# First batch of a fused attention and feed-forward kernel: k as fp32 over two hardware queues with casts on chip, first q in token quarters, v in three pieces

## The chip, the cores and the metric

One core of one Trainium2 chip. The metric is the device time of one execution in microseconds (us). Each kernel was run several times beside the kernel before on the same chip. The program runs on one core. A profiled span is about 1.8 us shorter than the device time of the same run.

## The reference, cut to what matters

```python
k_proj = np.einsum('ks,bhsd->bhkd', E, k)            # 64 projected rows per head
v_proj = np.einsum('ks,bhsd->bhkd', F, v)
scores = scale * np.matmul(q, k_proj.transpose(0, 1, 3, 2))
attn   = softmax(scores)
x      = np.matmul(attn, v_proj)                     # then heads side by side: (8192, 512)
g      = x @ w_gate                                  # 512 x 1536
out    = (g * sigmoid(g) * (x @ w_val)) @ w_out
```

There are 8 batches of 8 heads, 1024 tokens and head size 64, all fp32. The attention of a batch is small; the feed-forward matmuls make up 87% of the chain that ended last in the kernel before. It can't begin before the first batch has gone through projection, scores, softmax and the product with v.

## The kernel before

The kernel works in bf16. From the second batch on, attention is laid in between the feed-forward matmuls. The first batch has no such cover: k, q and v are loaded and cast by the Pool queue's transfers, and dummy matmuls on zeros (`warm`) keep the tensor engine running while they land.

```python
load_k(0, 0, 4)                      # Pool queue: fp32 in memory, bf16 in the tile
... E and F on the sync queue ...
load_k(0, 4, 8)
load_q(0, 0, 2)                      # heads 0-3, heads 4-7
load_v(0, (0, 4, 8))                 # two halves
load_w_gv(0, 1); load_w_gv(1, 2); load_w_gv(2, 4)
warm(8); turn(0); turn(1)            # turn: transpose E, then F, on the tensor engine
warm(7)
u_KV(0, "k", (0, 4), at="y")         # project k, heads 0-3
... u_KT: transpose it into the block-diagonal BD ...
u_KV(0, "k", (4, 8), at="y")
u_KT(0, at="v", prs=(2, 4))
u_T(0, 0, ...); u_T(0, 1, ...); u_T(0, 2, ...)     # transpose q
u_S(0, 0, "g"); ... u_S(0, 3, "a")   # scores and exp (exp on ACT)
u_R(0, 0); u_N(0, 0); ...            # row sums (DVE), products (Pool, two on DVE)
u_KV(0, "v", (0, 4), at="y")         # project v; BDV casts on ACT
u_A(0, 0, nc.scalar)                 # transpose the attention rows
...
u_KV(0, "v", (4, 8), at="y")
u_PV2(0, 0, 0, 0, nc.scalar); u_PV2(0, 0, 1, 0, nc.vector)   # product with v, xT copies
u_A(0, 1, nc.scalar); u_A(0, 3, nc.vector)
f_mm(0, 0, 0, 0)                     # first feed-forward matmuls, half width
```

The softmax here doesn't subtract the row's maximum and nothing guards it: scores larger than these inputs give would overflow.

## Time and profile before

| | kernel before |
|---|---|
| device time | 573.26 us (572.66 to 573.53, 4 runs) |
| tensor engine busy | 98% of a span of 572.4 us |
| second set of scores starts | 16.05 us |
| last piece of v lands | 20.0 us |
| first feed-forward matmul | 22.57 us |
| first gate matmul of full width ("the front") | 26.88 us |

The prediction below shows the lines. Two positions in the trace serve as rulers. The second score set (the first two sets together need all of k, and the attention transposes need both) says how the score chain does. The front, the first gate matmul with 512 columns, is where the tensor engine goes over to unbroken work; the rest of the span after it was 545.5 us here. The profiled run of the kernel before was one of its slower ones (574.16 us), 0.9 us above its median; if that lies ahead of the front, its front is late by as much.

### The profile page before, as it was taken

The page shows a single profiled execution, that of the slowest core. Times are in us where ns is not written, and L with a number is a line of the kernel's source. Part 1 is how long each engine was busy: PE and PEld are TensorE (multiplying, and loading weights), DVE is VectorE, ACT ScalarE, POOL GpSimd, SP SyncE. Part 2 cuts the span into 40 slices and gives each one's busy share as a digit, 9 for nine tenths or more (in the row PEclk, how much of TensorE's full clock was granted, in tenths as well). Part 3 has the DMA queues.
Part 4 walks back from the last instruction along what each step waited for, and adds up shares of the span by engine and source line. Part 5 has one row for each costly group of instructions (what it writes and reads, how often), then busy time and mean ns, then how long its engine had stood idle before and what let it go on. Part 6 is the DMA issues. An engine that isn't in the chain of part 4 may idle for free.

```text
span 572.4 us, 7867 instructions
## 1 busy us (share of the span) xinstructions
PE 561.2 (98%) x2910; PEld 268.6 (47%) x2967; DVE 336.8 (59%) x580; ACT 237.0 (41%) x416; POOL 107.9 (19%) x121
## 2 busy tenths in 40 slices
PE   8899999999999999999999999999999999999997
PEld 4654544444444444444444444444444444444444
DVE  2787566666466744766556665567546674554550
ACT  1655444353425434444335434354342543443232
POOL 6734131234002400124001330023200220000000
PEclk9999999999999999999999999999999999999999
DMA  9999993539901698037951399204990124100012
GB/s 160 196 200 206 201 161 74 93 64 196 201 37 41 110 190 157 18 75 129 187 108 38 59 179 195 63 22 88 197 176 37 42 52 74 38 37 25 31 39 92
DMA packets 105927, 61.34 MB, mean 107 GB/s; under 512 B 58016, under 2 KB 97696, under 8 KB 105888
## 3 DMA queue, kind: packets, MB, share of 16 engines
q0 software_dynamic: 42288, 29.89, 36.1%
q1 hardware_dynamic: 63312, 30.68, 25.1%
q8 instruction: 23, 0.38, 0.3%
q10 hardware_dynamic: 288, 0.26, 0.1%
q14 instruction: 16, 0.13, 0.1%
HBM read 60.29 MB, written 16.78 MB: 135 GB/s over the span
## 4 chain that ended last, share of the span: by engine, by line
PE 94%; DMA 2%; POOL 1%; ACT 1%; issue 1%; DVE 0%; POOLq 0%
PE yps L360 29%; PE vps L322 29%; PE gps L322 29%; PE kvp L147 3%; PE sc L227 2%; DMA vb<-in_v_dram 2%; PE pv L285 2%; PE aTp L274 0%; ACT xT L135 0%; PE qTp L193 0%; POOL kb L88 0%; PE kTp L172 0%; POOL qb L107 0%; ACT th L334 0%; PE pv L300 0%
## 5 line engine op out<-in xcount | busy, mean ns | idle before, releaser
L341 DVE SCALAR_TENSOR_TENSOR s<-th,gps 128x512 f32<-128x512 f32 x192 | 130.5, 680 | 138.0 <-ACT th L334 137.8
L322 PE MATMUL gps<-xT,wg 128*128 128x512 bf16 (+1 forms) x755 | 195.7, 377 | 1.2
L322 PE MATMUL vps<-xT,wv 128*128 128x512 bf16 (+1 forms) x761 | 195.9, 377 | 0.8
L360 PE MATMUL yps<-wo,hT 128*128 128x512 bf16 (+2 forms) x761 | 191.5, 376 | 0.8
L334 ACT ACTIVATE th<-gps 128x512 f32<-128x512 f32 x192 | 114.6, 597 | 162.6 <-PE gps L322 155.1
L346 DVE TENSOR_TENSOR hT<-s,vps 128x512 bf16<-128x512 f32 x192 | 132.0, 688 | 22.1 <-PE vps L322 1.5
L360 PEld LDWEIGHTS <-hT 128*128 128x128 bf16 x780 | 76.2, 98 | 89.9
L258 POOL TENSOR_TENSOR AAd<-ee,rr 128x512 bf16<-128x512 f32 x52 | 54.1, 1040 | 319.5 <-issue 168.4
L322 PEld LDWEIGHTS <-wv 128*128 128x128 bf16 x776 | 73.9, 98 | 82.9 <-issue 3.3
L322 PEld LDWEIGHTS <-wg 128*128 128x128 bf16 x776 | 74.0, 98 | 81.3 <-issue 0.6
L370 ACT ACTIVATE ysb<-yps 128x512 f32<-128x512 f32 (+1 forms) x65 | 38.4, 590 | 78.1 <-PE yps L360 74.4
L135 ACT CAST xT<-pv 128x512 bf16<-128x512 f32 x62 | 36.1, 585 | 51.3 <-PE pv L285 50.3
L242 DVE TENSOR_REDUCE zz<-ee 128x8 f32<-128x512 f32 x64 | 43.5, 679 | 17.9 <-ACT ee L231 17.9
L231 ACT ACTIVATE ee<-sc 128x512 f32<-128x512 f32 x64 | 37.9, 595 | 17.4 <-PE sc L227 17.4
L285 PE MATMUL pv<-AT,BDV 128*128 128x512 bf16 x60 | 22.6, 379 | 0.1
L227 PEld LDWEIGHTS <-qTd 128*128 128x128 bf16 x208 | 16.0, 98 | 12.3
L227 PE MATMUL sc<-BD,qTd 128*128 128x128 bf16 x208 | 20.1, 219 | 0.1
L135 DVE CAST BDV<-kvp 64x256 bf16<-64x256 f32 x14 | 6.0, 426 | 22.1 <-ACT ks L157 19.1
L258 POOL TENSOR_TENSOR AA<-ee,rr 128x512 bf16<-128x512 f32 x10 | 10.3, 1038 | 35.2 <-DVE rr L244 33.6
L147 PE MATMUL kvp<-kb,ET 128*64 128x512 bf16 (+1 forms) x72 | 15.5, 357 | 1.3 <-DMA kb<-in_k_dram 1.3
L244 DVE RECIPROCAL rr<-zz 128x8 f32<-128x8 f32 x64 | 13.0, 203 | 6.2
L147 PE MATMUL kvp<-vb,FT 128*64 128x512 bf16 (+1 forms) x72 | 15.5, 358 | 1.0 <-DMA vb<-in_v_dram 1.0
(49 smaller groups left out, 144.8 us busy)
## 6 DMA issues: line engine op xcount, KB each, us to landing
out_dram<-ysb SPq DMA_DIRECT2D x63, 256.0 KB, 2.3
qb<-in_q_dram POOLq DMA_DIRECT2D x15, 512.0 KB, 16.6
kb<-in_k_dram POOLq DMA_DIRECT2D x7, 1024.0 KB, 11.6
vb<-in_v_dram POOLq DMA_DIRECT2D x7, 1024.0 KB, 14.2
wo<-in_moe_w_out_dram POOLq DMA_DIRECT2D x2, 768.0 KB, 14.8
wg<-in_moe_w_gate_dram POOLq DMA_DIRECT2D x5, 256.0 KB, 10.4
wv<-in_moe_w_val_dram POOLq DMA_DIRECT2D x5, 256.0 KB, 10.4
kb<-in_k_dram POOLq DMA_DIRECT2D x2, 512.0 KB, 8.7
```

The costliest lines, as they stand in the source:

```text
L135: (nc.scalar.copy if eng is nc.scalar else eng.tensor_copy)(out=out, in_=in_)
L147: nc.tensor.matmul(out=t[lo : lo + 64, h0:h1].rearrange("p h d -> p (h d)"), lhsT=w[:, j, :], rhs=src[b][:, h0:h1, j, :], start=(j == 0), ...
L227: nc.tensor.matmul(out=ps[:, n, :], lhsT=t[:, n, :], rhs=BD[b % 2][:, 4 * g + n, :], start=True, stop=True)
L231: nc.scalar.activation(out=e[:].rearrange("p h j k -> p (h j k)"), in_=ps[:].rearrange("p a k -> p (a k)"), func=AF.Exp, scale=scale,)
L242: nc.vector.reduce_sum(out=z[:], in_=e[:], axis=AX.X)
L258: eng.tensor_tensor(out=a.rearrange("p j h k -> p h j k"), in0=ee.pop((b, u))[:], in1=rr.pop((b, u))[:].unsqueeze(3).to_broadcast([P, 4, 2 ...
L322: nc.tensor.matmul(out=ps[:, ts], lhsT=(wg, wv)[w][:, kt, f * P : (f + 1) * P], rhs=x[:, kt, ts], start=(kt == 0), stop=(kt == NKT - 1),)
L334: nc.scalar.activation(out=th[:], in_=ps[:], func=AF.Tanh, scale=0.5)
L341: nc.vector.scalar_tensor_tensor(out=s1[:], in0=th[:], scalar=1.0, in1=g[:], op0=ALU.add, op1=ALU.mult)
L346: nc.vector.tensor_tensor(out=hT[c][:, f, :], in0=s1[:], in1=ps[:], op=ALU.mult)
L360: nc.tensor.matmul(out=yy[c][:, cs], lhsT=hT[c][:, f, i * P : (i + 1) * P], rhs=wo[:, f, cs], start=(f == 0), stop=(f == NFT - 1),)
L370: nc.scalar.activation(out=ysb[:, cs], in_=yy[c][:, cs], func=AF.Copy, scale=0.5)
```

## The change

The intent, as far as the edit shows it, is to have the score chain ready earlier by bringing k first, over the hardware queues of the sync engine and ACT and not by the Pool (which was busy 0.94 and 0.76 us with issuing the two k transfers before), and to have less work left after the last piece of v. The core of the diff (cuts marked):

```diff
-        load_k(0, 0, 4)
-        ... E, F on nc.sync ...
+        nc.sync.dma_start(out=ef[0][:], in_=E)
+        load_k0(nc.scalar, 0)         # fp32, two heads each
+        load_k0(nc.sync, 1)
+        load_k0(nc.scalar, 2)
+        load_k0(nc.sync, 3)
+        nc.scalar.dma_start(out=ef[1][:], in_=F)
...
-        load_k(0, 4, 8); load_q(0, 0, 2); load_v(0, (0, 4, 8))
-        load_w_gv(0, 1); load_w_gv(1, 2); load_w_gv(2, 4)
+        load_q(0, 0, (0, 2)); load_v(0, (0, 4)); load_q(0, 0, (2, 4)); load_v(0, (4, 6, 8))
+        for f in range(2): load_w_gv(f, f + 1)
         warm(8)
         turn(0)
+        warm(4)
+        cast_k((0, dve), (1, dve), (2, dve), (3, act))
+        u_KV(0, "k", (0, 4), at="y")
+        cast_k((4, dve), (5, dve))
+        u_KT(0, at="v", prs=(0, 2))
+        u_T(0, 0, "a", act)
+        u_T(0, 2, "a", act)
+        cast_k((6, dve), (7, act))
+        warm(6)
+        u_KV(0, "k", (4, 8), at="y")
+        turn(1)
+        u_KT(0, at="v", prs=(2, 4))
+        u_S(0, 0, "g") ... u_S(0, 2, "g") ...
+        u_T(0, 1, "a", act); u_T(0, 3, "a", act)
+        u_KV(0, "v", (0, 4), at="y")  # now ahead of the third and fourth score sets
+        u_S(0, 1, "g"); ... u_A(0, 0, act); u_S(0, 3, "g") ...
+        load_w_gv(2, 4)               # now after the third softmax product
...
+        u_KV(0, "v", (4, 6), at="y")
+        warm(1)
+        u_KV(0, "v", (6, 8), at="y")
+        u_PV2(0, 0, 0, 0, act); u_PV2(0, 0, 1, 0, act)
...
+        f_mm(0, 0, 0, 0); u_A(0, 1, act); f_mm(0, 0, 1, 0); u_A(0, 3, dve)
```

More of the change, by code (lines that the diff above doesn't have):

```diff
@@ L85, in load_k @@
     def load_k(b, h0=0, h1=H):
-        if h0 == 0:
+        if b:
             kb[b] = kv_pool.tile([P, H, NJ, D], BF16, name="kb", tag="kb")
@@ L93, in load_v @@
     def load_v(b, heads=(0, H)):
-        t = kv_pool.tile([P, H, NJ, D], BF16, name="vb", tag="vb")
-        vb[b] = t
+        if heads[0] == 0:
+            vb[b] = kv_pool.tile([P, H, NJ, D], BF16, name="vb", tag="vb")
+        t = vb[b]
         for h0, h1 in zip(heads, heads[1:]):
@@ L100, in load_v, with load_q @@
             )
-    def load_q(b, ch, parts=1):
-        t = q_pool.tile([P, H, 4, D], BF16, name="qb", tag="qb")
-        qb[b, ch] = t
-        n = H // parts
-        for i in range(parts):
-            nc.gpsimd.dma_start(
-                out=t[:, i * n : (i + 1) * n].rearrange("p h j d -> p h (j d)"),
-                in_=q[b, i * n : (i + 1) * n].rearrange("h (p c j) d -> p c h (j d)", c=2, j=4)[:, ch],
-            )
+    def load_q(b, ch, js=(0, 4)):
+        if js[0] == 0:
+            qb[b, ch] = q_pool.tile([P, H, 4, D], BF16, name="qb", tag="qb")
+        js = slice(*js)
+        nc.gpsimd.dma_start(
+            out=qb[b, ch][:, :, js, :].rearrange("p h j d -> p h (j d)"),
+            in_=q[b].rearrange("h (p c j) d -> p c h j d", c=2, j=4)[:, ch, :, js, :].rearrange(
+                "p h j d -> p h (j d)"
+            ),
+        )
     def load_w_gv(c0, c1, which=(0, 1)):
@@ L426, with load_k0 @@
     with tc.manual_schedule():
-        load_k(0, 0, 4)
-        ef = []
-        for which, src in (("E", E), ("F", F)):
-            raw = const.tile([KP, S], FP32, name=f"{which}raw")
-            nc.sync.dma_start(out=raw[:], in_=src)
-            ef.append(raw)
+        kb[0] = kv_pool.tile([P, H, NJ, D], BF16, name="kb", tag="kb")
+        kraw = [
+            aw.tile([P, 2, NJ * D], FP32, name="kraw", tag=tag)
+            for tag in ("qTd", "AAd", "qTd", "AAd")
+        ]
+        ef = [const.tile([KP, S], FP32, name=f"{x}raw") for x in "EF"]
+        def load_k0(eng, i):
+            eng.dma_start(
+                out=kraw[i][:],
+                in_=k[0, 2 * i : 2 * i + 2].rearrange("h (p j) d -> p h (j d)", j=NJ),
+            )
+        nc.sync.dma_start(out=ef[0][:], in_=E)
[4 more added lines that the diff above has]
+        nc.scalar.dma_start(out=ef[1][:], in_=F)
         zeros = const.tile([P, CW], BF16, name="zeros")
@@ L461, in warm, with cast_k @@
                 )
-        load_k(0, 4, 8)
-        load_q(0, 0, 2)
-        load_v(0, (0, 4, 8))
-        load_w_gv(0, 1)
-        load_w_gv(1, 2)
-        load_w_gv(2, 4)
+        load_q(0, 0, (0, 2))
+        load_v(0, (0, 4))
+        load_q(0, 0, (2, 4))
+        load_v(0, (4, 6, 8))
+        for f in range(2):
+            load_w_gv(f, f + 1)
         warm(8)
         turn(0)
-        turn(1)
-        warm(7)
-        u_KV(0, "k", (0, 4), at="y")
-        warm(2)
-        u_KT(0, at="v", prs=(0, 2))
-        warm(2)
-        u_KV(0, "k", (4, 8), at="y")
-        warm(2)
+        warm(4)
+        def cast_k(*hs):
+            for h, eng in hs:
+                copy(eng, kb[0][:, h].rearrange("p j d -> p (j d)"), kraw[h // 2][:, h % 2])
+        dve, act = nc.vector, nc.scalar
+        cast_k((0, dve), (1, dve), (2, dve), (3, act))
[7 more added lines that the diff above has]
+        u_KV(0, "k", (4, 8), at="y")
+        turn(1)
         u_KT(0, at="v", prs=(2, 4))
-        u_T(0, 0, "a", nc.scalar)
-        u_T(0, 1, "a", nc.vector)
-        u_T(0, 2, "a", nc.scalar)
         u_S(0, 0, "g")
-        u_T(0, 3, "v", nc.vector)
+        warm(1)
         u_S(0, 2, "g")
-        u_S(0, 1, "a")
-        u_S(0, 3, "a")
         u_R(0, 0)
@@ L492 @@
         u_N(0, 2)
-        load_w_gv(4, 6, (0,))
+        warm(1)
+        u_T(0, 1, "a", act)
+        u_T(0, 3, "a", act)
         u_KV(0, "v", (0, 4), at="y")
+        warm(2)
+        u_S(0, 1, "g")
         warm(1)
-        u_A(0, 0, nc.scalar)
+        u_A(0, 0, act)
+        u_S(0, 3, "g")
+        warm(2)
         u_R(0, 1)
         u_N(0, 1)
+        load_w_gv(2, 4)
+        u_A(0, 2, act)
         u_R(0, 3)
         u_N(0, 3)
-        u_A(0, 2, nc.scalar)
-        u_KV(0, "v", (4, 8), at="y")
-        load_w_gv(4, 6, (1,))
+        u_KV(0, "v", (4, 6), at="y")
+        warm(1)
+        u_KV(0, "v", (6, 8), at="y")
+        u_PV2(0, 0, 0, 0, act)
+        u_PV2(0, 0, 1, 0, act)
+        load_w_gv(4, 6)
         load_q(0, 1)
-        load_w_gv(6, 8)
-        load_w_gv(8, 10)
-        load_w_gv(10, 12)
+        for f in (6, 8, 10):
+            load_w_gv(f, f + 2)
         load_wo(0)
@@ L510 @@
         load_k(1)
-        warm(1)
-        u_PV2(0, 0, 0, 0, nc.scalar)
-        u_PV2(0, 0, 1, 0, nc.vector)
-        u_A(0, 1, nc.scalar)
-        u_A(0, 3, nc.vector)
         f_mm(0, 0, 0, 0)
+        u_A(0, 1, act)
         f_mm(0, 0, 1, 0)
-        u_PV2(0, 0, 0, 1, nc.scalar)
-        u_PV2(0, 0, 1, 1, nc.vector)
+        u_A(0, 3, dve)
         f_mm(0, 1, 0, 0)
+        u_PV2(0, 0, 0, 1, act)
+        u_PV2(0, 0, 1, 1, dve)
         f_mm(0, 1, 1, 0)
```

## The prediction

> **What bounds the kernel now.** I read the page's busy shares first, then the time slices, the chain of waits over the first 32 us, the timeline of the same stretch, and each transfer's time from issue to landing.
>
> ```profile
> PE 561.2 (98%) x2910; PEld 268.6 (47%) x2967; DVE 336.8 (59%) x580; ACT 237.0 (41%) x416; POOL 107.9 (19%) x121
> PE   8899999999999999999999999999999999999997
> ```
>
> TensorE (PE) is busy for 98% of the span, and from the third slice on every slice is full. No other engine bounds the body. What can still be won lies in the ramp before the tensor engine has real work without a break, and the change touches only that ramp. The timeline shows where it ends:
>
> ```profile
> 22.57 0.73 PE L322 MATMUL gps<-xT,wg 128*128 128x256 bf16 x4
> ...
> 26.88 1.02 PE L322 MATMUL gps<-xT,wg 128*128 128x512 bf16 x3
> ```
>
> The first feed-forward matmul starts at 22.57 us of a span of 572.4 us. Everything after it, 572.4 - 22.57 = 549.8 us, is the same work in both kernels. So the question is how much earlier that matmul comes, and whether the advance is kept. The chain of waits says what set 22.57:
>
> ```profile
> 3.99 1.49 POOL qb L107 x2
> 5.48 0.70 POOL vb L97
> 6.18 13.83 DMA vb<-in_v_dram
> 20.01 0.04 issue
> 20.05 1.07 PE kvp L147 x8
> ```
>
> It is one transfer: the second half of v lands at 20.0, then 8 projection matmuls (1.07 us), two BDV casts on ACT (0.26 and 0.27), PV and the xT copy follow. A busy count of PE before 20 us misleads here: 23 of those matmuls are dummies on zeros that only keep it running. The windows view (engine columns are busy us and counts, then clock, DMA share in us, GB/s written) shows that the transfers were not at full rate at first:
>
> ```profile
> 4.00:6.00 2.00, 1.95 (x11) 1.10 (x10) 0.00 (x0) 0.52 (x2) 2.00 (x3) 1.00 1.08 168
> 6.00:8.00 2.00, 1.92 (x13) 1.39 (x14) 0.85 (x2) 0.22 (x1) 2.00 (x4) 1.00 1.11 140
> 8.00:10.00 2.00, 0.96 (x7) 0.46 (x5) 0.00 (x0) 0.00 (x0) 0.45 (x2) 1.00 1.09 175
> ...
> 26.00:28.00 2.00, 1.85 (x13) 1.07 (x12) 1.75 (x3) 0.77 (x3) 1.40 (x2) 1.00 1.45 197
> ```
>
> From 4 to 10 us the mean is (168 + 140 + 175) / 3 = 161 GB/s against a steady 197. These are bf16 bytes written; the fp32 bytes read are twice that, 394 GB/s. The last lines show how close the second wait is, the scores that need all of k:
>
> ```profile
> 12.29 1.03 PE L147 MATMUL kvp<-kb,ET 128*64 128x256 bf16 x8 [0.27 <-DMA kb<-in_k_dram]
> 15.20 0.39 PE L227 MATMUL sc<-BD,qT 128*128 128x128 bf16 x4
> 21.97 0.76 PE L274 MATMUL aTp<-ident_bf,AA 128*128 128x128 bf16 x8
> ```
>
> **What the Trainium skill says.** "DMA: Bandwidth & Descriptors", section "Issuing engines are not separate DMA queues": transfers issued by different engines share the same 16 DMA engines, so more queues save issue time, not bandwidth. The trace agrees as far as it goes: once full, the single Pool queue holds 195 to 206 GB/s written, about 400 read, and I expect no more in the new kernel. The same page, section "Latency and other measured facts", puts the first byte of a hardware-queue transfer at about 0.6 us and of a Pool one at about 1 us. Here E on the sync queue landed 3.7 us after issue (256 KB), the first k half on the Pool 8.5 us (512 KB): the direction agrees, the sizes are much larger. Its table "Specifications" says that transfers need 512 B or more for line rate; this agrees with the windows at 18 to 20 us (some of the 128-column weights, 256 B written per row), with a DMA share of 1.65 of 2 us for 183 GB/s against 1.45 for 197; the quartered q now has such rows. "VectorE: DVE Perf Modes", section "Mode 2×_2P — use both read ports for one tensor", says a plain fp32 copy in SBUF makes two results per cycle. No such cast is in this trace (the f32 casts of 512 from PSUM took 0.69); my estimate with the page's 0.96 GHz is 512 / 2 / 0.96 = 0.27, with overhead 0.35 us per head.
>
> **The change part by part.** (1) k moves from the Pool queue to two hardware queues: 2.10 MB fp32 with E and F of 0.26 MB each, 2.62 MB. I expect first bytes at about 2.5 us. Needed before the last v piece lands are E, F, k (2.62), half of q (1.05) and v (2.10), 5.77 MB; at 394 GB/s that is 14.6 us, so v would land at 2.5 + 14.6 + 0.9 (completion, my allowance) = 18.0 instead of 20.0. That equals repairing the 4 to 10 us stretch, 6 x (197 - 161) / 197 = 1.1 us, plus 0.9 from the start.
> (2) k's landing. If the hardware queues get all of the rate, 2.62 / 0.394 = 6.6 us, landed at 9.1; if the Pool's q and v take a third, 10.0 us, 12.5. I choose 10 for the last k piece. Two casts, the slower on ACT, 0.6; projection 1.03; the F transposes that now stand in between, 1.09 (a row of 8 in the old timeline); k transposes 0.23; four BD copies 0.22 each, 0.9; hand-overs 0.2. The second score set starts at 14.1, against about 16.05. From there to the finished first AT half the old trace needs 20.27 - 16.05 = 4.2 us, so 18.3.
> (3) Last v piece of 2 heads, not 4: its 8 matmuls have 128 columns instead of 256, 1.03 becomes about 0.5; BDV casts 0.53 becomes about 0.4.
> (4) Added on the path: both first xT copies are now on ACT, 2 x 0.59 one after the other, where one was on DVE alongside: about 0.5 us. Eight k casts are added, six on DVE and two on ACT, 6 x 0.35 + 2 x 0.6 = 3.3 engine us, nearly all of it while k is still landing. Dummy matmuls rise from 23 to 26, 0.22 to 0.24 us each, mostly inside waits.
> Sum: v at 18.0 + 0.5 + 0.4 + 0.2 (PV) + 0.6 to 1.2 (xT) = 19.7 to 20.3. The weights of the first column block follow v on the queue, 0.52 MB at about 0.36, 1.45 us, so 19.5. First feed-forward matmul at about 20.2, **2.4 us earlier**.
> (5) Given back: weight blocks 2 to 3 were issued at 13.93 and 15.21, ahead of the softmax products on the Pool. Now they are issued after two such products (1.04 us each), at perhaps 17.5 to 19, and took 10.4 us in the old trace with a full queue. With the queue nearly empty I expect about 5 us. They are needed about 4.3 us after the first matmul (26.88 - 22.57), at 24.5. An idle stretch of the DMA of up to 1 us also moves every later weight back. I charge 0.8 us. Net 1.6 us.
>
> **The rivals.** A, **k does not come earlier**: the Pool transfers are interleaved with it and it lands at 12 or later, or the first q (now behind the identity set-up on the Pool) holds the tensor engine, which is in order. The chain k, cast, F transposes, BD then gives scores at 16 as before, v's advance is hidden, and the time is 573.0 to 573.8. For it: the F transposes and six dummies in the path; against it: six dummies would hardly be put there if k were not awaited at that point. B, **the weights become the wait**: issue of blocks 2 to 3 falls behind, the matmuls stall at block 2 or 6, and the gain shrinks to 0.5 us or less, 572.9. For it: the old trace lands blocks 6 to 7 of wv at 33.59 and uses them at 34.87, only 1.3 us of slack; against it: all transfers start earlier. C, **everything is kept**: k at 9, no DMA gap, gain 2.5 to 3 us, 570.4 to 570.9.
>
> **Range and chances.** From 573.39 less 1.6 I say 571.8. A's bad end is 573.8 and C's good end 570.4; eight in ten between 570.3 and 573.3. Two per cent is 11.5 us. The time before the first feed-forward matmul is 22.57 us in all, and half of it would have to vanish for a gain of 2%, while the first bytes alone take over 2 us and 14.6 us of transfers must follow. A loss of 11 us would need a stall of half the ramp. So: faster 0.01, same 0.98, slower 0.01.
>
> **What would show it right or wrong.** Step 1: the DMA near 200 GB/s written (about 400 while fp32 k moves) from 3 to 10 us, v landing near 18. Step 2: last k piece near 10, the second score set near 14. Sum: first feed-forward matmul near 20.2. Step 5: waits of that matmul's line on wg or wv after 24 us, and a dip in the DMA before. If scores start at 16, A is right; if the first matmul is early but the time from it to the end is over 551 us, B. I am wrong if hardware queues are slower on 2 KB rows of fp32 than the Pool's casting transfers, which this trace does not show, or if quartered q lands last of all.

## The result, and the profile after

The changed kernel takes 579.48 us (579.21 to 580.55, 4 runs) against 573.26 us: slower by 6.2 us, ratio 1.0113 with a 95% interval of 1.0096 to 1.0131. A ratio here is the mean time of one kernel's fast runs over the mean of the other's fast runs of the same rounds, so it isn't quite the ratio of the medians.

The page of the changed kernel, its busy line and the row of the granted clock:

```profile
PE 567.4 (98%) x2978; PEld 269.6 (47%) x2978; DVE 338.0 (59%) x583; ACT 239.8 (42%) x423; POOL 107.3 (19%) x120
PEclk7999999999999999999999999999999999999999
```

The busy share is 98% as before and says nothing; the first digit of the clock row, 7 where every other is 9, says that the ramp ran for a time on a slower clock. The chain of waits of the first 32 us no longer begins with v but with k:

```profile
1.37 8.50 DMA kraw<-in_k_dram
9.87 0.02 issue
9.90 0.63 ACT kb L137
10.53 0.04 issue
10.57 1.88 PE kvp L149 x8
...
14.14 1.45 PE warm L474 x6
15.59 0.99 PE kvp L149 x8
16.58 0.60 PE efp L462 x4
```

The first projection waits for the second k piece (1.37 + 8.50 = 9.87) and its cast on ACT. Then six dummies (`warm`), the second projection and the F transposes (`efp`) stand on the path one after another. The windows of the changed kernel (columns as in the prediction) show the clock and the transfers:

```profile
4.00:6.00 2.00, 0.50 (x2) 0.00 (x0) 0.93 (x2) 0.00 (x0) 2.00 (x4) 1.00 1.00 274
6.00:8.00 2.00, 1.89 (x11) 1.39 (x12) 0.00 (x0) 0.74 (x2) 2.00 (x3) 0.87 1.10 367
8.00:10.00 2.00, 0.78 (x2) 0.00 (x0) 0.10 (x1) 0.10 (x1) 0.10 (x1) 0.50 1.12 262
12.00:14.00 2.00, 1.54 (x14) 1.03 (x12) 0.75 (x4) 0.61 (x2) 0.74 (x1) 0.50 1.24 207
22.00:24.00 2.00, 1.92 (x22) 1.29 (x20) 1.53 (x3) 1.99 (x5) 0.55 (x1) 1.00 0.00 0
```

The tensor engine is busy for only 0.50 and 0.78 of 2 us in two stretches. The clock (the figure ahead of the last two) falls to 0.50 near 7.5 us, after the first of them, and stays there through the second until 14.3; 0.87 is the mean of a window in which it fell. At 22 to 24 us nothing is transferred at all. The timeline gives the two rulers, the last k cast and the first feed-forward matmul:

```profile
14.71 0.63 ACT L137 CAST kb<-kraw 128x512 bf16<-128x512 f32 x1
...
18.97 0.33 PE L229 MATMUL sc<-BD,qT 128*128 128x128 bf16 x3 [0.28 <-DVE BD L183]
...
24.29 0.60 PE L149 MATMUL kvp<-vb,FT 128*64 128x128 bf16 x8 [0.38 <-ACT BDV L137]
...
26.02 0.86 PE L324 MATMUL gps<-xT,wg 128*128 128x256 bf16 x4 [0.32 <-ACT xT L137]
...
31.24 1.02 PE L324 MATMUL gps<-xT,wg 128*128 128x512 bf16 x4
```

The second score set runs at 18.97 instead of 16.05 (one of its four matmuls already ran at 18.47; the other three wait for the last copy into BD). The first feed-forward matmul comes at 26.02, where the prediction's sum said 20.2 and the kernel before has 22.57, and the front at 31.24 instead of 26.88, 4.4 us late. Of these 4.4, 2.9 are there at the second score set; the other 1.4 arise between it and the front, a stretch of 12.27 us here and 10.83 before. The last v piece landed near 18.9 (issue near 5.15, 13.7 to landing) and is first used at 24.29: v isn't the wait any more, by 5.4 us. The loss is all ahead of the front: from there to the end it is 577.4 - 31.24 = 546.2 us, against 545.5.

### The profile page after: what moved, and what is told of

It is laid out like the page before. It is cut to its first block, busy times and chain, and to the rows that moved or that the text cites. A ratio compares the mean times of both kernels' runs of the same rounds, so it can differ in the third digit from the quotient of the medians.

```text
span 577.4 us, 7963 instructions
## 1 busy us (share of the span) xinstructions
PE 567.4 (98%) x2978; PEld 269.6 (47%) x2978; DVE 338.0 (59%) x583; ACT 239.8 (42%) x423; POOL 107.3 (19%) x120
## 4 chain that ended last, share of the span: by engine, by line
PE 94%; ACT 2%; DVE 2%; DMA 1%; issue 0%; SPq 0%; DVEq 0%
PE yps L362 29%; PE gps L324 28%; PE vps L324 28%; PE kvp L149 3%; PE sc L229 2%; PE pv L287 2%; DMA kraw<-in_k_dram 1%; ACT xT L137 1%; ACT th L336 0%; PE qTp L195 0%; DVE s L343 0%; PE warm L474 0%; DVE hT L348 0%; ACT ee L233 0%; DVE zz L244 0%
## 5 line engine op out<-in xcount | busy, mean ns | idle before, releaser
L324 PE MATMUL gps<-xT,wg 128*128 128x512 bf16 (+1 forms) x776 | 198.2, 377 | 0.7 <-ACT xT L137 0.3
L362 PE MATMUL yps<-wo,hT 128*128 128x512 bf16 (+1 forms) x780 | 194.6, 376 | 0.0
L229 PEld LDWEIGHTS <-qTd 128*128 128x128 bf16 x208 | 16.0, 98 | 12.3
L149 PE MATMUL kvp<-kb,ET 128*64 128x512 bf16 (+1 forms) x72 | 16.3, 373 | 1.8 <-ACT kb L137 1.8
L149 PE MATMUL kvp<-vb,FT 128*64 128x512 bf16 (+2 forms) x80 | 15.7, 339 | 0.4 <-ACT BDV L137 0.4
## 6 DMA issues: line engine op xcount, KB each, us to landing
kb<-in_k_dram POOLq DMA_DIRECT2D x7, 1024.0 KB, 11.5
vb<-in_v_dram POOLq DMA_DIRECT2D x7, 1024.0 KB, 14.1
```

The lines of the kernel that those rows point to most:

```text
L149: nc.tensor.matmul(out=t[lo : lo + 64, h0:h1].rearrange("p h d -> p (h d)"), lhsT=w[:, j, :], rhs=src[b][:, h0:h1, j, :], start=(j == 0), ...
L229: nc.tensor.matmul(out=ps[:, n, :], lhsT=t[:, n, :], rhs=BD[b % 2][:, 4 * g + n, :], start=True, stop=True)
L324: nc.tensor.matmul(out=ps[:, ts], lhsT=(wg, wv)[w][:, kt, f * P : (f + 1) * P], rhs=x[:, kt, ts], start=(kt == 0), stop=(kt == NKT - 1),)
L362: nc.tensor.matmul(out=yy[c][:, cs], lhsT=hT[c][:, f, i * P : (i + 1) * P], rhs=wo[:, f, cs], start=(f == 0), stop=(f == NFT - 1),)
```

## The experiments

Fifteen kernels (there is no e4), all correct. CLOCK, ORDER, DELIVERY and so on are theories of where the 6.2 us went. "Second scores" and "front" are read from each run's one profiled execution, the time is a median, the ratio is against the kernel before.

| run | what it is | time, us | ratio (95%) | second scores | front |
|---|---|---|---|---|---|
| changed | | 579.48 | 1.0113 (1.0096 to 1.0131) | 18.97 | 31.24 |
| e1 | 13 more dummies | 577.97 | 1.0077 (1.0064 to 1.0090) | 17.88 | 30.15 |
| e2 | k pieces 1, 2 exchanged | 578.15 | 1.0079 (1.0065 to 1.0093) | 18.25 | 30.52 |
| e3 | second projection ahead of q | 580.20 | 1.0121 (1.0106 to 1.0137) | 18.85 | 31.12 |
| e5 | early weights | 580.28 | 1.0115 (1.0101 to 1.0129) | 20.58 | 32.85 |
| e6 | e1, two copies off ACT | 577.58 | 1.0071 (1.0057 to 1.0084) | 18.04 | 30.27 |
| e7 | e1 with e3's order | 576.60 | 1.0053 (1.0040 to 1.0065) | 16.38 | 28.65 |
| e8 | e1, F transposes in a wait | 576.96 | 1.0063 (1.0051 to 1.0076) | 17.00 | 29.27 |
| e9 | e7, v tail in one projection | 576.68 | 1.0059 (1.0045 to 1.0073) | 16.62 | 28.11 |
| e11 | e9, early weights | 575.63 | 1.0039 (1.0027 to 1.0051) | 16.56 | 28.06 |
| e10 | e9, k by the Pool | 575.55 | 1.0044 (1.0032 to 1.0057) | 16.07 | 27.56 |
| e12 | e10, early weights, early F | 575.33 | 1.0037 (1.0021 to 1.0053) | 14.05 | 27.25 |
| best1 | combined | 574.32 | 1.0020 (1.0008 to 1.0033) | 15.10 | 26.95 |
| b1 | before, v in three | 575.04 | 1.0023 (1.0010 to 1.0035) | 15.44 | 28.50 |

(In the rows from the changed kernel to e10, "second scores" is the start of the set's last three matmuls; in e12 and best1 it is that of the whole set, and in b1, as in the kernel before, that of a merged row that holds it, so these read up to half a microsecond early beside the others. best2 and best3 follow below. Rows come from different rounds, in which the kernel before itself had medians from 573.15 to 573.57.)

### e1_clock: hold the clock

```diff
-        warm(8)
+        warm(12)
         turn(0)
-        warm(4)
+        warm(13)
```

> The changed kernel with 13 more dummy matmuls in its two early waits (12 instead of 8 before the E transposes, 13 instead of 4 after them), nothing else. CLOCK theory: the drop of the tensor clock to half from 7.7 to 14.3 us stretched the first k projection (1.86 instead of 1.03), the q transposes (1.04 instead of 0.62) and the six dummies (1.65 instead of 1.3), about 1.6 us on the path; with the clock held, the projection takes about 1.03, the first feed-forward matmul comes at about 24.4 instead of 26.0 and the time falls to about 577.9. ORDER theory (the second k half waits for its casts, which stand behind the q transposes, and these wait for q landing at 12.3): the path hardly moves, 579.0 or more.

577.97 us, 1.5 us less, with nothing but more work added in waits.

```profile
10.70 1.03 PE L149 MATMUL kvp<-kb,ET 128*64 128x256 bf16 x8 [0.19 <-ACT kb L137]
...
30.15 1.02 PE L324 MATMUL gps<-xT,wg 128*128 128x512 bf16 x3
```

The first projection starts no earlier (10.70) and takes 1.03 instead of 1.86. CLOCK is right for 1.5 of the 6.2 us by the medians (1.1 at the front of the two profiled runs, 2.1 by the ratios); the rest has another cause.

### e2_k1_act: which queue brings which piece

```diff
-        load_k0(nc.sync, 1)
-        load_k0(nc.scalar, 2)
+        load_k0(nc.scalar, 1)
+        load_k0(nc.sync, 2)
```

> The changed kernel with k pieces 1 and 2 exchanged between the two hardware queues, so that the ACT queue brings pieces 0 and 1 and SP brings E, 2 and 3. DELIVERY theory: the first projection waited for piece 1, which landed at 9.87 us while piece 2 had landed at about 7.6; with the exchange piece 1 lands near 7.6, the projection starts near 8.3 instead of 10.57, the idle stretch is too short for the clock to fall, and the time falls by about 2 us to 577.5. ORDER theory: the second half of k still comes at 10.9 and the q quarter at 12.3, so the scores move by under 0.5 us and the time stays at 579 or more.

578.15 us, 1.3 us less. The first projection starts at 9.14, and then it doesn't help as expected:

```profile
9.14 1.79 PE L149 MATMUL kvp<-kb,ET 128*64 128x256 bf16 x8
12.75 0.62 PE L195 MATMUL qTp<-ident_bf,qb 128*128 128x128 bf16 x8 [1.14 <-DMA qb<-in_q_dram]
14.83 1.03 PE L149 MATMUL kvp<-kb,ET 128*64 128x256 bf16 x8 [0.16 <-ACT kb L137]
```

The tensor engine now waits 1.14 us for q, which stands in program order ahead of the second projection, and that one starts 0.7 us earlier only. The clock fell here too (1.79 for the first projection) but was back by 12.75, so part of the 1.3 us is the clock's: from the q transposes to the second projection e2 needs 2.08 us and the changed kernel 2.41. So DELIVERY was half right: piece 1 was late because the sync queue brought it, but earlier arrival of the first half of k is mostly swallowed behind q.

### e3_order and e7_order_warm: the second half of k ahead of q

e3 moves the second projection and the casts of heads 6 and 7 ahead of the q transposes and drops the six dummies. e7 does this with the clock held; all casts come ahead of the first projection.

```diff
         cast_k((0, dve), (1, dve), (2, dve), (3, act))
+        cast_k((4, dve), (5, dve), (6, dve), (7, act))
         u_KV(0, "k", (0, 4), at="y")
-        cast_k((4, dve), (5, dve))
+        warm(2)
         u_KT(0, at="v", prs=(0, 2))
+        u_KV(0, "k", (4, 8), at="y")
         u_T(0, 0, "a", act)
         u_T(0, 2, "a", act)
-        cast_k((6, dve), (7, act))
-        warm(6)
-        u_KV(0, "k", (4, 8), at="y")
         turn(1)
```

> The changed kernel with the casts of heads 6 and 7 and the second k projection moved ahead of the first two q transposes, and the six dummies between them taken out. ORDER theory: the last k piece landed at 10.9 but was cast only at 14.2 to 15.3 because the casts stood behind the q copies; the second projection starts at about 13 instead of 15.5, the second score set comes about 2 us earlier than 18.97 and the time falls to about 577.4. CLOCK theory: the path shortens by the dummies alone at most (1.45 us), and what remains still runs at half clock; about 578.2.

> The clock-held kernel (577.97 us) with all casts ahead of the first k projection in program order, the second k projection ahead of the q transposes, and the five to six dummies between them reduced to two. ORDER theory: the second projection starts near 12.4 instead of 14.45 and the second score set near 16.3 instead of 17.9, time about 576.4. Rival (q is the wait): q landed at 12.3, so the transposes move up to it only if the second projection is not in front; the score set moves by under 0.5 us, 577.5 or more. Rival (clock): with fewer dummies the clock falls again and the run is like the unwarmed reordering, 579 or more.

e3 alone gave nothing: 580.20 us. Its trace shows why, and a trap besides. This is its first projection in the timeline:

```profile
10.74 1.87 PE L149 MATMUL kvp<-kb,ET 128*64 128x256 bf16 x8 [1.82 <-ACT kb L137]
```

and this the window that it lies in:

```profile
10.00:12.00 2.00, 1.26 (x7) 1.17 (x8) 1.47 (x4) 0.62 (x1) 0.00 (x0) 1.00 1.48 252
```

Eight matmuls that take 1.03 at full clock took 1.87, as did the second projection, while the clock column says 1.00. In that run the record missed the drop; the durations show it (e5's trace has the same: 1.86 at a shown 1.00). Without the dummies the engine stayed slow for longer, and that ate what the order gave: in the other three runs of e3 the mean clock of the span is 0.987 to 0.988, in those of the changed kernel 0.991 to 0.994. With the clock held, e7, the same order gives 576.60 us, 1.4 below e1:

```profile
12.38 1.06 PE L149 MATMUL kvp<-kb,ET 128*64 128x256 bf16 x8
16.38 0.33 PE L229 MATMUL sc<-BD,qT 128*128 128x128 bf16 x3 [0.28 <-DVE BD L183]
```

The second projection comes at 12.38, expected 12.4, the scores at 16.38, expected 16.3. ORDER is right, for 1.4 us, and its test needed the clock as a control.

### e8_turn: the F transposes inside a wait

```diff
-        warm(6)
+        turn(1)
         u_KV(0, "k", (4, 8), at="y")
-        turn(1)
```

> The clock-held kernel (577.97 us) with the 8 transposes of F put in place of the six dummies, ahead of the second k projection. ORDER theory: 1.09 us leaves the path between the second projection and the scores; the second score set comes at about 16.9 instead of 17.9, time about 577.0. ACT or DVE theory: what follows is set by those engines after the scores, and the time stays within 0.3 us of 577.97.

On top of e1: 576.96 us, 1.0 us less; the scores at 17.00. The F transposes, which the change put on the path, cost about 0.9 of their 1.09 us there. No run adds this edit to e7 alone; the two gains probably overlap, since both fill the same wait.

### e5_w24, e9_onev, e11_w24: weights and the tail of v

```diff
         for f in range(2):
             load_w_gv(f, f + 1)
+        load_w_gv(2, 4)
...
-        load_w_gv(2, 4)              # after the third softmax product
```

> The changed kernel with weight blocks 2 to 3 issued right after blocks 0 and 1, as before, instead of after the third softmax product. WEIGHTS theory (rival B of the prediction): the transfers stood idle from about 22 to 26 us and that is given back later, so the time falls by 1 us or more, to 578.4 or less. The other theories: no matmul after 26 us waits on a weight, the early issue changes nothing, 579.2 to 579.7.

580.28 us: no gain. In its profiled run k came later still (first projection at 11.30), but from its front to the end it is 578.7 - 32.85 = 545.9 us against 546.2, so early weights are worth 0.3 us at most here. The 4 us in which nothing was transferred cost the changed kernel nothing: what they bring was used later still.

e9 takes e7 and projects the last four heads of v at once.

```diff
-        u_KV(0, "v", (4, 6), at="y")
-        warm(1)
-        u_KV(0, "v", (6, 8), at="y")
+        u_KV(0, "v", (4, 8), at="y")
```

> The clock-held and reordered kernel (e7, 576.60 us) with the last four heads of v projected in one piece again; the transfers of v stay in three. TAIL theory: v landed near 18.9 and the tail is used only at about 20.4, so splitting it saves nothing and costs a second round between the tensor engine and ACT (the last projection waits 0.38 for the BDV casts of the one before it): first feed-forward matmul about 0.8 us earlier than 23.44, time about 575.8. Rival (the short tail is worth what it was meant for): the single piece costs about 0.5 us more, 577.0.

The front comes 0.54 us earlier, 28.11, so the split tail was a cost. But the time stays at 576.68. The trace of e9 has a line that none of the runs before it has:

```profile
35.59 1.04 PE L324 MATMUL gps<-xT,wg 128*128 128x512 bf16 x4 [0.41 <-DMA wg<-in_moe_w_gate_dram]
```

A gate matmul of block 6 waits for weights. e11 issues blocks 2 to 3 early on top of e9:

> e9_onev with weight blocks 2 to 3 issued right after blocks 0 and 1, as in the kernel before. NEW-WAIT theory: in e9_onev the front came 0.54 us earlier than in e7 and the time did not fall, because the gate matmuls of block 6 waited on their weights (0.41 us in one place of the trace); issued early, the blocks keep ahead and the time falls by about 0.6 to 0.9 us, to about 575.9. Rival: the tail of e9_onev was longer for another reason, and the time stays within 0.2 us of 576.7.

575.63 us, 1.05 below e9, and no such wait; from the front to the end it is 545.7 us instead of 546.6. The same edit was worth nothing in e5 and 1 us here: what a late transfer costs depends on how early its user comes. e9 and e11 together are worth 1.0 us against e7.

### e6_act: ACT after the scores

On top of e1, the last copy of q and one xT copy go to DVE, and two transposes of q move ahead of the second softmax product.

```diff
         u_N(0, 0)
+        u_T(0, 1, "a", act)
+        u_T(0, 3, "a", dve)
         u_R(0, 2)
         u_N(0, 2)
         warm(1)
-        u_T(0, 1, "a", act)
-        u_T(0, 3, "a", act)
...
-        u_PV2(0, 0, 1, 0, act)
+        u_PV2(0, 0, 1, 0, dve)
```

> The clock-held kernel (13 more dummies, 577.97 us) with two copies taken off ACT: the copy of the fourth q transpose and the second xT copy go to DVE. ACT theory: from the first scores to the first feed-forward matmul ACT carries some 7 us of work in 8 us where the kernel before gave it 5, so ACT sets that stretch; two copies of 0.53 less bring the first full-width gate matmul (30.15) 0.8 to 1 us forward, time about 577.1. ORDER theory: that stretch is set by the order on the tensor engine and by DVE, the copies only move; 577.7 or more.

Between the first exp and the second xT copy ACT is busy for 7.1 of 8.2 us in the changed kernel, against 5.0 of 6.4 us in the kernel before (up to its one xT copy on ACT), which made it a suspect. Taking two copies of 0.53 each off it gave 577.58 us, 0.4 less, which the overlapping intervals don't set apart from nothing, and no earlier front in the profiled run (30.27; from the second scores 12.23 us against 12.27). The theory fell in that form: the first gate matmul still waits 0.32 us for the first xT copy, and the second, now 0.69 us on DVE, ends no earlier.

### e10_kpool: k by the Pool again

e9 with the k loads of the kernel before and no casts.

```diff
-        nc.sync.dma_start(out=ef[0][:], in_=E)
-        load_k0(nc.scalar, 0) ... load_k0(nc.sync, 3)
-        nc.scalar.dma_start(out=ef[1][:], in_=F)
+        load_k(0, 0, 4)
+        nc.sync.dma_start(out=ef[0][:], in_=E)
+        nc.sync.dma_start(out=ef[1][:], in_=F)
...
+        load_k(0, 4, 8)
         load_q(0, 0, (0, 2))
```

> The same as e9_onev, but k of the first batch comes as before: two halves on the Pool queue, cast in the transfer, no casts on DVE and ACT, E and F both on SP; order on the tensor engine and q quarters unchanged. Theory that the hardware queues bring little: k half two lands at about 12.2 instead of cast at about 11.7, q at about 13.7 instead of 12.3, so the scores come about 0.3 to 1 us later than with the hardware queues and the time is 0 to 1 us above e9_onev. Rival (hardware delivery itself is the cost): the time is lower than e9_onev by 1 us or more.

575.55 us, 1.1 below e9 although it has e9's wait on weights too (0.34 us at 34.97). Four of its five runs lie below all five of e9. Here the second k half landed at 3.23 + 7.7 = 10.9 us, in bf16 and ready to use. The hardware queues' last piece landed near 11.5 in the changed kernel (issued near 2.0, 9.5 to landing; the expectations of e2 and e3 had misread this as 10.9), and still had to be cast, so it could be ready near 12.1. The Pool's landing varies, though: the same two transfers had the second half in at 12.25 in the trace of the kernel before, 11.62 in b1, 10.63 in e12 and 12.10 in best3. What the runs show is that the main part of the change brings the second half of k no earlier than within that spread; that the hardware queues are slower isn't shown, since in e9 the Pool's q and v share the DMA engines with k and in e10 they stand behind it. The second projection starts at 12.06 in e10, 12.62 in e9. I had expected e10 to be the slower of the two.

### b1_v3: v in three pieces, alone

The kernel before with three v transfers and a split last projection.

```diff
-        load_v(0, (0, 4, 8))
+        load_v(0, (0, 4, 6, 8))
...
-        u_KV(0, "v", (4, 8), at="y")
+        u_KV(0, "v", (4, 6), at="y")
+        u_KV(0, "v", (6, 8), at="y")
```

> The kernel before with one part of the change alone: v in three pieces, the last of two heads. Theory that the part is good in itself: the last v landing (20.0) set the first feed-forward matmul, and 8 projection matmuls of 128 columns take 0.6 instead of 1.07, so the time falls by about 0.5 us, to about 573.0 against the kernel before in the same rounds. Rival: one more Pool transfer and an extra pair of cast instructions take it back, or the tail is hidden by the softmax chain: within 0.2 us.

575.04 us, slower by 0.23% (interval 0.10 to 0.35%), not faster.

```profile
19.88 0.63 PE L147 MATMUL kvp<-vb,FT 128*64 128x128 bf16 x8
21.06 0.96 PE L147 MATMUL kvp<-vb,FT 128*64 128x128 bf16 x8 [0.55 <-ACT BDV L135]
```

The last projection waits 0.55 us for the BDV casts of the piece before: both pieces are columns of one PSUM tile, and the program orders a write to it behind the reads. The two projections and the wait between them stretch over 2.1 us, where one of 1.07 stood. The engine was also slow again after the wait (0.96 for work of 0.63; the granted clock is 0.50 from 21.15 to 24.56), and the three runs at clock 1.000 (573.75 to 575.04) are faster than the two at 0.997 (575.13 and 575.80). How much of the loss is the wait's and how much the clock's isn't separated.

### e12_fw, best1, best2, best3: putting it together

e12 takes e10 with weights 2 to 3 early and F transposed right after E. best1 keeps the change's parts (k by hardware queues, q quarters) and repairs what was found.

e12 against e10:

```diff
+        load_w_gv(2, 4)
         warm(12)
         turn(0)
-        warm(13)
+        turn(1)
+        warm(7)
...
-        turn(1)
...
-        load_w_gv(2, 4)              # after the third softmax product
```

best1 against the changed kernel (cut: dummies moved, and the last two attention transposes ahead of the first feed-forward matmul):

```diff
-        load_k0(nc.sync, 1); load_k0(nc.scalar, 2)
+        load_k0(nc.scalar, 1); load_k0(nc.sync, 2)
-        load_v(0, (4, 6, 8))
+        load_v(0, (4, 8))
-        warm(8); turn(0); warm(4)
+        warm(12); turn(0); warm(6)
...                                   # project k, heads 0-3; casts 4, 5
+        turn(1)
         cast_k((6, dve), (7, act))
+        u_KT(0, at="v", prs=(0, 2)); warm(1)
-        warm(6)
         u_KV(0, "k", (4, 8), at="y")
-        turn(1)
+        u_T(0, 0, "a", act); u_T(0, 2, "a", dve)
...                                   # scores and products of sets 0 and 2
+        load_w_gv(2, 4)
         u_KV(0, "v", (0, 4), at="y")
+        u_T(0, 1, "a", act); u_T(0, 3, "a", dve)
...
-        u_KV(0, "v", (4, 6), at="y"); warm(1); u_KV(0, "v", (6, 8), at="y")
+        u_KV(0, "v", (4, 8), at="y")
-        u_PV2(0, 0, 1, 0, act)
+        u_PV2(0, 0, 1, 0, dve)
```

> e10_kpool (k on the Pool queue, 575.55 us) with two more parts of the kernel before put back: F transposed right after E (six dummies fewer), and weight blocks 2 to 3 issued early. If the F transposes (1.09 us), the late weights (0.6) and the late first projection (10.37 because of its dummies, 9.4 possible) are what is left of the loss, the time falls by 1.5 to 2.2 us to about 573.7. If the q quarters or the order after the scores are a cost of their own, 574.5 or more.

> All that the runs pointed to in one kernel: k pieces 0 and 1 first on the ACT queue, the F transposes right after the first k projection, casts ahead of the copies that wait for q, v tail in one piece, copies shared between ACT and DVE, dummies only where something is awaited. If these causes add up, the first k projection starts near 9, the second near 11.7, the second score set at 14.4 instead of 18.97, v landing near 18.9 sets the first feed-forward matmul at about 21, and the time is about 572.5 (572.0 to 573.3), at or just below the kernel before. If the hardware delivery or the clock costs something that is not yet named, 574 or more.

e12: 575.33 us with a wide spread (574.49 to 577.49; the two slowest are the two at clock 0.997), against an expected 573.7. Its scores come at 14.05, two us before those of the kernel before, and its front at 27.25: the lead is lost between them. Its chain of waits begins with the second piece of q:

```profile
16.12 0.62 PE L195 MATMUL qTp<-ident_bf,qb 128*128 128x128 bf16 x8 [1.26 <-DMA qb<-in_q_dram]
16.67 1.06 PE L149 MATMUL kvp<-vb,FT 128*64 128x256 bf16 x8
```

That piece is issued behind the first half of v, at 5.61, and lands at 16.07; in the kernel before all of this q is in at 14.93, and its four score sets follow one another from 15.20 to 16.89. The record thus points at the part of the change that no experiment takes back, q in token quarters with v between them, which every version but b1 keeps. e12's expectation had named it: with a time of 574.5 or more, "the q quarters or the order after the scores are a cost of their own".

best1: 574.32 us, 5.2 us below the changed kernel, and 0.20% above the kernel before with an interval that excludes zero.

```profile
8.93 1.06 PE L149 MATMUL kvp<-kb,ET 128*64 128x256 bf16 x8
12.40 1.03 PE L149 MATMUL kvp<-kb,ET 128*64 128x256 bf16 x8 [0.49 <-ACT kb L137]
...
18.60 0.40 PE L229 MATMUL sc<-BD,qT 128*128 128x128 bf16 x4 [0.68 <-ACT qT L137]
...
26.95 1.02 PE L324 MATMUL gps<-xT,wg 128*128 128x512 bf16 x4
```

The first projection comes 0.8 us before that of the kernel before (9.74; 0.2 before that of b1, 9.12), the second at 12.40, where the kernel before has 12.29 and b1 11.66. What arrives earlier isn't what the scores wait for. After that, the second set (15.10) and the last v (landed at 19.03) are both about 1 us earlier than in the trace of the kernel before, and the front isn't. best1's chain of waits runs not through v but through its third and fourth score sets (18.60 and 19.06), their exp and softmax, and the attention transposes that it put ahead of the first feed-forward matmul; its second piece of q landed only at 16.54, and the transposes of it then stood behind the first v projection until 17.30. Two attempts at the stretch after the scores followed. best2 is best1 with the first two attention transposes ahead of the third and fourth score sets and both late q copies on DVE:

```diff
-        u_T(0, 1, "a", act)
-        u_T(0, 3, "a", dve)
-        u_S(0, 1, "g")
+        u_T(0, 1, "v", dve)
+        u_T(0, 3, "v", dve)
         u_A(0, 0, act)
-        u_S(0, 3, "g")
         u_A(0, 2, act)
+        u_S(0, 1, "g")
+        u_S(0, 3, "g")
```

> best1 (574.32 us) with the first two attention transposes ahead of the third and fourth score sets, and both late q copies on DVE. ACT theory: in best1 the tensor engine waited 0.68 us for a q copy on ACT in front of the attention transposes, and ACT finished their copies only at 21.09 with v landed at 19.04; with this order the BDV casts follow v, the first full-width gate matmul comes 0.4 to 0.7 us before 26.95 and the time is about 573.7. Rival (v and its own chain set it): within 0.2 us of 574.3.

574.59 us (ratio 1.0020, 1.0007 to 1.0033): no gain; its profiled run fell on a slow stretch of the tensor engine (1.36 for the second projection) and says little. best3 is e12 with the attention transposes ahead of the q transposes, weights 2 to 3 after the first products, and the second xT copy on DVE:

```diff
-        load_w_gv(2, 4)              # ahead of the first dummies
...                                   # after the first two products
+        load_w_gv(2, 4)
-        u_T(0, 1, "a", act); u_T(0, 3, "a", act)
         u_KV(0, "v", (0, 4), at="y")
+        u_A(0, 0, act); u_A(0, 2, act)
+        u_T(0, 1, "v", act); u_T(0, 3, "v", dve)
         u_S(0, 1, "g")
-        u_A(0, 0, act)
         u_S(0, 3, "g")
         u_R(0, 1); u_N(0, 1)
-        u_A(0, 2, act)
         u_R(0, 3); u_N(0, 3)
...
-        u_PV2(0, 0, 1, 0, act)
+        u_PV2(0, 0, 1, 0, dve)
```

> e12_fw (575.33 us, k on the Pool queue) with the first two attention transposes ahead of the q transposes that wait for the last q quarter (landed at 16.1 there), weight blocks 2 to 3 issued after the first softmax products instead of before them, and the second xT copy on DVE. HEAD-OF-LINE theory: in e12_fw the second score set came at 14.05, two us before that of the kernel before, and the lead was lost because the attention transposes stood behind the q transposes (a wait of 1.26 us for q) and the first product behind a weight transfer on the Pool; with both moved the first full-width gate matmul comes near 26.2 instead of 27.25 and the time is about 574.0. Rival: v, landed near 18.7, and the ACT copies after it set the front in any order; within 0.3 us of e12_fw.

576.09 us (ratio 1.0049, 1.0036 to 1.0061), worse than e12. The attention transposes came at 18.17 and not earlier, the third and fourth scores slipped to 20.22, and the first gate matmul then waited 0.72 us for an xT copy on DVE that stood behind a softmax product. My head-of-line theory for e12 isn't confirmed; nor is its trace a clean test, since its transfers landed later than e12's (second half of k 12.10 against 10.63, last v 20.10 against 18.68). The last 1.1 us between best1 and the kernel before is left open. The q quarters and the later third and fourth score sets are the candidates that the traces name; a run with q in two halves of heads ahead of v, as before, would test them. No version beat the kernel before.

## Why the prediction was wrong, point by point

It said 571.8 us, 1.6 faster; the change cost 6.2.

**What bounds the kernel** was right: only the ramp moved. From front to end the two profiled runs differ by 0.7 us of a total of 5.0.

**Step 1, the transfers,** was mis-sized. It took 394 GB/s for fp32 over hardware queues; the four windows from 2 to 10 us show 309, 274, 367 and 262, a mean of 303. Still v landed near 18.9 where 18.0 was predicted. Those 0.9 us don't matter, because v had stopped being the wait.

**Step 2, k's landing, is the step that failed.** It said "the second score set starts at 14.1"; it starts at 18.97. By its terms: last k piece predicted at 10, measured near 11.5 (1.5 late). Then "two casts, the slower on ACT, 0.6": the cast begins at 14.71 and ends at 15.34, so in place of 0.6 there are 3.9 us. The sum let the cast begin when its data landed. On ACT it stood behind the copies of the q transposes, on DVE behind the copies into BD, and these stood on the tensor engine behind the first projection, which waited for piece 1 until 10.57. e7 puts the casts and the second projection forward and gets 1.4 us of that back. The rest of the sum held: from the end of the cast to the scores it has 3.45 us, and the trace 3.63 (projection 1.06 for 1.03, F transposes 1.09 for 1.09). So 1.5 late, 3.3 of waiting behind other work and 0.2 make the 4.9 us. The sum also had no term for the clock: it took every tensor duration from a trace at full clock, though the change put new waits in the ramp. e1 measures that term, 1.5 us; part of it lies inside the 3.3.

**Step 3, the short v tail,** had the right duration (0.60 for 0.5 predicted) and the wrong sign: v wasn't the bound, and splitting added a wait between tensor engine and ACT (e9, front 0.54 us earlier without it, though its scores come 0.24 later; b1, 1.3 us slower alone, a part of it by the clock).

**Step 4, the added work:** the two xT copies on ACT take 1.07 together, as priced, but the charge of 0.5 us on the path was too high: from the start of the first to the end of the second it is 1.08, where ACT and DVE in the kernel before took 1.15 (21.71 to 22.86). e6, which moves one back to DVE, agrees. The k casts took 0.42 to 0.43 us on DVE in most cases for 0.35 estimated, and 0.62 to 0.63 on ACT for 0.6.

**Step 5, the weights,** were charged 0.8 us and cost nothing in the changed kernel (e5). The mechanism was right and appeared as soon as the front advanced: e9 to e11, 1.05 us, at block 6, which rival B had named.

**The rivals.** A came nearest: k at 11.5 with its casts late, scores after 16. But A bounded its loss at 573.8, since it let the scores fall back only to the old time. It lacked the two things that made them later than before: a slower clock and a longer program order ahead of them. B fell for the changed kernel and C fell altogether.

The account: 1.5 us clock (e1), 1.4 us order around the second half of k (e7), 1.0 us split v tail and late weights together (e9, e11), 1.3 us from e11 to best1, which bundles the first-half delivery, the F transposes in a wait and shared copies, and 1.1 us open; the steps add up to the 6.2 by construction and so don't check one another. Each carries a few tenths, as the medians are from different rounds. These are steps in one order of repair; in another order they would split differently, as e8's 1.0 us beside e7 shows.

## What to carry to other kernels

When a sum of durations says when something will be ready, put in each term the later of "its data has landed" and "its engine, in program order, has got to it"; a cast or copy emitted behind something that waits inherits that wait. Before crediting earlier delivery of a part, ask whether it is the part that is waited for last: in best1 the first half of k came somewhat earlier and the second didn't, and in the changed kernel neither was used earlier. And a new wait ahead of tensor work can cost more than its own length, so hold the clock fixed with dummies before testing any other theory. Last, take back every part of a change once: here the part that wasn't, the q quarters, is what the open end points to.

## What the Trainium skill lacked or had wrong

- "TensorE: Matmul & The Clock Gate", "Part 1: The HAM clock gate", says that the array falls to half clock after at least one idle window of about 3.4 us. In the changed kernel no single wait was that long: 1.59 us before 6.09, then only the E transposes and part of four dummies before the granted clock fell to 0.50 near 7.5 us; a second wait, 1.79 before 10.57, came while it was low, and it was back at 14.3. The stretches at 0.50 last 6.8 us here and 3.4 in e2 and b1. How much idleness short of a whole window is enough isn't stated there; the kernel before with one wait of 1.04 in that region kept full speed.
- The same section warns that the recorded clock events can be unreliable. The reordered kernel's windows show 1.00 while eight matmuls took 1.87 us instead of 1.03. The 1.00 isn't to be trusted at the start either: the first eight dummies of the kernel before take 3.59 us under it, seven later ones 1.67. The page names a throttle-time counter to check against, which these profiles don't show; comparing the same matmuls' durations was the test here.
- "DMA: Bandwidth & Descriptors", "Issuing engine by pattern", calls the hardware queues generally faster. Here 2.62 MB of fp32 over two of them had its last piece at about 11.5 us, with a mean of 303 GB/s in the windows, while the Pool's casting transfers brought the same k complete at 10.6 to 12.25 us in five traces. From 2 to 10 us of e10 the Pool wrote 1.03 MB of bf16 beside 0.52 MB of E and F, read from 2.58 MB: 323 GB/s. For the whole of k no run here shows the hardware queues to be faster, nor, since q and v ran beside them, that they are slower.
- The same page, "Issuing engines are not separate DMA queues", says that transfers interleave. That section doesn't say how unevenly: from 2 to 10 us of the changed kernel the two hardware queues wrote 1.30 and 1.07 MB and the Pool's 0.06. The ACT queue's second k piece (issued near 1.3) landed near 7.5, the sync queue's first (issued at 1.37) at 9.87, behind E on its queue, and the Pool's 256 KB quarter of q, issued at 1.76, at 12.3.
